# Moving output stores to another queue, and three smaller edits, in a planned attention and gated-convolution kernel

## The chip, the cores and the metric

The kernel runs on one core of a Trainium2 chip. The metric is the device time of one execution in microseconds (us); smaller is better. A core has the engines TensorE (PE; its weight loads are shown as PEld), VectorE (DVE), ScalarE (ACT), GpSimd (POOL) and SyncE (SP), each with its own queue of instructions that it takes strictly in order. SP, ACT and POOL also issue DMA transfers. The names SPq and POOLq stand for these queues.

## The reference

Two stages. The first is causal attention with a forgetting gate for 8 batches, 8 heads, 576 positions and head size 64:

```python
scores = scale * np.matmul(q, k.transpose(0, 1, 3, 2))
cum = np.cumsum(np.log(np.clip(f, 0.0001, 1.0)), axis=-1)
decay = cum[:, :, :, None] - cum[:, :, None, :]
scores = np.where(causal, -1000000000.0, scores + decay)
attn = softmax(scores);  x = attn @ v      # then (B, S, H * D) = (8, 576, 512)
```

The second is a gated feed-forward with a convolution over the sequence, 512 to 1024 to 512, for each batch:

```python
h = np.maximum(x @ w_in, 0.0)              # w_in 512 x 1024
conv_out = conv_w[0] * h[s-1] + conv_w[1] * h[s] + conv_w[2] * h[s+1]
out = (h * sigmoid(conv_out)) @ w_out      # w_out 1024 x 512
```

## The kernel before

**Units of work.** Attention goes by half batches `hb` of 4 heads (16 of them) and inside them by pairs `i` of 2 heads (32). For a half batch, `load_qk` (L110) loads Q and K with DMA transposes into tiles `stq` and `stk`, a ring of four: half batch `hb` takes the tile of `hb - 4` and waits until PE has used it. V is loaded in five transfers (`load_v`, L158). The tiles hold 16-bit halves of the fp32 inputs, and some of their partitions are used for other things: constants are put there by `fill` (L132) with DMAs from a tile of constants, and the cumulated log of the gate, the decay, as a high and a low bf16 part (`rows_of`, L139 and L141). The decay rows come from `kd`, a copy in DRAM of the tiles `khi_sb` and `klo_sb`, which hold one row for each head. `clamp` (L119) on DVE prepares other partitions; for Q of half batches from `CLAMPS` = 8 on, an additional fill of 48 rows takes the place of that clamp.

For each pair PE computes the scores (L293, with mask matmuls L299 and L325), ACT the exponentials (L305, L319, L333), PE the product with V ("PV", L351), and DVE the normalized result `xn` (`norm`, L362 and L364). When a batch's four pairs are through, `xn` is transposed to `xt`: for batches 0, 1 and 7 on PE (`xpose_pe`, L397, copied out of PSUM by ACT or DVE, L406 and L408), for the others by five DMA transposes on SP (`xpose`, L383).

The feed-forward goes by batch `g` and block `ff` of 128 of the 1024 inner columns: L420 on PE, `relu` (L433) on ACT, two steps of the convolution (L450, L452) on DVE, `tanh` or for the last batch sigmoid (L462, L460) on ACT, `gate` (L470, L468) on DVE. The second matmul (L482) takes chunks of 128 positions, nine for two batches. A chunk's result is put into an output buffer `ob` by ACT or DVE (`evac`, L506, L508); a buffer holds two chunks, and there are three buffers. `store` (L515, L517) writes them to the output with DMAs on SP. For the last batch the second matmul runs block by block into banks that attention no longer needs (`moe2_last`, L495); two chunks of the batch before it (those from `HELD` = 2 on) are computed after that.

**The order of the work.** Nothing reorders instructions at run time. A planner writes the order: each unit is a `task` with engines and estimated times, the tasks it comes after, a key (its due time), the ring or buffer that it takes and gives back, a lag until others may use its result, and DMA time. `play()` runs through an estimated clock and lets each engine take the ready task with the smallest key; the kernel is then emitted in that order. A task's give-back was counted 0.1 us after its issue, for DMAs too. `AHEAD` (4.0) limits how far score tasks may run ahead of the feed-forward, `QUEUED` (8.0) how much estimated DMA time SP may have queued.

```python
z = task({"SP": 0.55}, [x], key, lambda g=g, c=c, n=1 if single else 2: store(g, c, n),
         give=[("ob", y if c % 2 else x)] if c % 2 or c == 8 else [], lag=2.0, ...)
...
if give:
    heapq.heappush(heap, (end + 0.1, k, "give"))
```

**Weights.** `w_in` (L630) and `w_out` (L150) are loaded by POOL. So that they don't come too early, a store of one element by DVE (`hold`, L146) into the destination makes the DMA wait for it.

Of the kernel before, what the change touches and what calls it, by code (L numbers as in the profile page):

```python
# [18 lines left out]
def kernel(  # L19
# [115 lines left out]
    def rows_of(hb):  # L135

        tq, tk = stq_t[hb % RING], stk_t[hb % RING]
        c = slice(hb * HH, (hb + 1) * HH)
        nc.gpsimd.dma_start(tq[126:127, 0:HS], kd[0:1, c, :].rearrange("j h s -> j (h s)"))  # L139
        row = HS + 64  # L140
        nc.gpsimd.dma_start(bass.AP(tensor=tk.tensor, offset=int(tk.offset) + 96 * row, ap=[[2 * row, 2], [1, HS]]),  # L141
                            kd[:, c, :].rearrange("j h s -> j (h s)"))

    def hold(w):

        nc.vector.memset(w[0:1, 0, 0:1], 0.0)  # L146
# [360 lines left out]
        else:  # L507
            nc.vector.tensor_scalar(ob, ps, by, None, op0=ALU.mult)  # L508

    def store(g, c, n):  # L510

        r = (g - g % 2) * S + 128 * (c + 1 - n)
        ob = ob_of[g, c - c % 2]
        if n == 1:
            nc.sync.dma_start(outf[r:r + 128, :], ob[:, c % 2, :])  # L515
        else:
            nc.sync.dma_start(outf[r:r + 256, :].rearrange("(j p) c -> p j c", p=128), ob)  # L517

# [19 lines left out]
        nc.vector.memset(z[0:2, :], PAIR)  # L540
        nc.vector.memset(z[32:33, :], MINUS)

    CLAMPS, HALVES, LANDING = 8, 16, 3.0
    HELD = 2
    WAITS = ((3, 0), (3, 1), (4, 0), (4, 1))
    room = {"sc": 2, "O": 1, "mm": 2, "pm": 2, "xn": 2, "xt": 2, "u": 2, "ht": NHT,
            "hg": 2, "ob": 3}
# [7 lines left out]
    for hb in range(NHB):  # L555
# [4 lines left out]
        for s in range(2):  # L560
            if hb == 1:
                x = task({"ACT": 0.01}, [], -9, lambda: None, lag=(0.3, 3.8)[s])
            elif hb:
                last = x = task({"SP": 3.0}, ring, key + 0.1 * s, lambda hb=hb, s=s: load_qk(hb, 0, 4, s),
                                lag=LANDING, dma=3.1, behind=last)
            if hb:
                landed.append(x)
            if hb:
                t = (stq_t, stk_t)[s][hb % RING]
                rows = [(100, 14, 19)] if s else [(96, 15, 0)] + [(0, 48, 33)] * (hb >= CLAMPS)  # L570
                even.append(task({"POOL": 0.55 * len(rows)}, [t_fsrc, x], 2 * hb - 3.5,
                                 lambda t=t, rows=rows: [fill(t, *x) for x in rows],
                                 lag=4.0, dma=0.3 if s or hb < CLAMPS else 1.2))
            if hb and (s or hb < CLAMPS):
                even.append(task({"DVE": 0.9}, [x], (2 * hb - 3 if hb > 1 else -5) + 0.2 * s,
                                 lambda hb=hb, s=s: clamp(hb, s, 0, 4, 96)))
# [12 lines left out]
                x = task({"DVE": 0.1}, [even[1] if side == 0 else even[-1]], -9, lambda j=j: hold(w_out_f16[:, 2 * j:2 * j + 2, :]))  # L589
                t_wout.append(task({"POOL": 0.8}, [x], 2 * hb - 1.0, lambda j=j: load_w_out(j), lag=2.0, dma=1.7))  # L590
        if hb:
            t_rows[hb] = even + [task({"POOL": 1.1}, landed, 2 * hb - 3.6 if hb > 1 else -1.0,
                                      lambda hb=hb: rows_of(hb), lag=3.8)]
        else:
            t_rows[hb] = []
        for p in range(2):
# [4 lines left out]
        for p in range(2):  # L601
            i = 2 * hb + p
            if i == 1:
                t_rows[hb] = [t_second]
            if p == 0:
                x = t_second = task({"ACT": 0.01}, [], -9, lambda: None, lag=3.7) if i == 0 else None
                t_tail = x = task({"PE": 0.36}, t_rows[hb] + [x] * (i == 0), i + (0.02 if i else 0.65),
                                  lambda hb=hb: tail_scores(hb), take="sc")
                tail = task({"ACT": 0.36}, [x] + ([t_pv[i - 3, 1]] if hb >= 2 else []), i + 0.02,
                            lambda hb=hb: tail_exp(hb), give=[("sc", x)])  # L610
            exps = {}
            x = task({"PE": 0.9}, t_rows[hb], i + 0.1, lambda i=i: diag_scores(i), take="sc")
            t_qk[hb, p] = [t_tail, x]
            mask = task({"ACT": 1.02}, [x], i + 0.1, lambda i=i: diag_exp(i), take="pm", give=[("sc", x)])
            for s in range(2):
                x = task({"PE": 0.46}, t_rows[hb], i + 0.2 + 0.4 * s, lambda i=i, s=s: off_scores(i, s),
                         take="sc")
                t_qk[hb, p].append(x)
                exps[s] = task({"ACT": 1.02}, [x] + ([t_pv[i - 2, s]] if i >= 2 else []), i + 0.2 + 0.4 * s,
                               lambda i=i, s=s: off_exp(i, s), give=[("sc", x)])  # L620
            for s in range(2):
                t_pv[i, s] = task({"PE": 0.5}, [exps[s], mask, tail, t_cast[hb, 0], t_cast[hb, 1]]
                                  + ([t_pv[i, 0]] if s else []), i + 0.9 + 0.4 * s,
                                  lambda i=i, s=s: pv(i, s), take="O" if s == 0 else None,
                                  give=[("pm", mask)] if s else [])
            t_norm[i] = task({"DVE": 1.05}, [t_pv[i, 1]], i - 0.5, lambda i=i: norm(i),
                             take="xn" if i % PPB == 0 else None, give=[("O", t_pv[i, 0])])
            if i == 0:
                x = task({"DVE": 0.1}, [t_norm[0]], -9, lambda: hold(w_in_f16))
                t_win = task({"POOL": 1.0}, [x], -0.5, lambda: nc.gpsimd.dma_start(  # L630
                    w_in_f16, moe_w_in.rearrange("(cc p) ff -> p cc ff", p=128)), lag=2.0, dma=6.5)
        if hb % 2:
            norms = [t_norm[i - j] for j in range(PPB)]
            if b in (0,1,7):
                t_xt[b] = []
                for tb in range(NKB):
                    x = task({"PE": 0.27}, norms, i + 0.3 + 0.1 * tb, lambda b=b, tb=tb: xpose_pe(b, tb),
                             take="mm", also="xt" if tb == 0 and grp_of[b][1] == 0 else None, behind=x if tb else None)
                    if tb == 0:
                        t_xt0[b] = x  # L640
                    t_xt[b].append(task({"DVE": 0.4, "ACT": 0.57}, [x], i, lambda e, b=b, tb=tb: xpose_out(b, tb, e),
                                        give=[("mm", x)] + ([("xn", t_norm[i - 3])] if tb == NKB - 1 else [])))
            else:
                t_xt0[b] = task({"SP": 7.0}, norms, i + 0.5, lambda b=b: xpose(b),
                                take="xt" if grp_of[b][1] == 0 else None,
                                give=[("xn", t_norm[i - 3])], lag=2.8, dma=3.1)
                t_xt[b] = [t_xt0[b]]
# [5 lines left out]
    for g, (b0, nb) in enumerate(GROUPS):  # L653
# [3 lines left out]
        for ff in range(NFF):  # L657
# [16 lines left out]
            if ff == 0 and g % 2 == 0:  # L674
                t_hg = x
            t_tanh.append(x)
            t_gate[g, ff] = task({"DVE": 0.1 + n / 1800.0 if g == LAST else 0.2 + n / 1050.0}, [x], key - 1.5, lambda g=g, ff=ff: gate(g, ff),
                                 give=[("ht", t_m1[-nt])])
        t_exp = t_tanh if g == LAST - 1 else []
        done = [t_gate[g, ff] for ff in range(NFF)]  # L680
# [12 lines left out]
        for c in chunks:  # L693
            key = start[g + 1] + (start[g + 2] - start[g + 1]) * (c - chunks[0]) / len(chunks) + 5.0
            if g == LAST:
                x = t_m2[0] if t_m2 else x
            else:
                late = g == LAST - 1 and c >= HELD
                x = task({"PE": 1.73}, done + t_wout, key + 99 * late, lambda g=g, c=c: moe2(g, c), take="mm")
                if late:  # L700
                    t_late.append(x)
            t_m2.append(x)
            x = task({"DVE": 0.62, "ACT": 0.57}, [x] + ([y] if c % 2 else []), key - 2.0,
                     lambda e, g=g, c=c: evac(g, c, e), give=[("mm", x)] if g < LAST else [], take="ob" if c % 2 == 0 else None)
            single = c == 8 or g >= LAST - 1
            if c % 2 or single:
                z = task({"SP": 0.55}, [x], key, lambda g=g, c=c, n=1 if single else 2: store(g, c, n),
                         give=[("ob", y if c % 2 else x)] if c % 2 or c == 8 else [], lag=2.0, dma=0.45 if single else 0.9)
            y = x
        if g % 2:  # L710
            task({"SP": 0.01}, t_m2, key, lambda: None, give=[("hg", t_hg)])

    AHEAD, QUEUED = 4.0, 8.0

    def play():
        busy = {"PE": 11.5, "ACT": 12.0, "DVE": 12.0, "POOL": 14.0, "SP": 19.0}
# [16 lines left out]
        while len(started) < len(tasks):  # L733
# [11 lines left out]
            for e in ("PE", "ACT", "DVE", "POOL", "SP"):  # L745
# [3 lines left out]
                while ready[e]:  # L749
# [27 lines left out]
                    end = clock + engines[e]  # L777
                    busy[e] = end
                    heapq.heappush(heap, (end, -1, None))
                    if give:  # L780
                        heapq.heappush(heap, (end + 0.1, k, "give"))
                    if dma:
                        dma_free = max(dma_free, clock) + dma
                        end = max(end, dma_free) if e == "SP" else end + 2.5 + dma
                    heapq.heappush(heap, (end + lag, k, "done"))
                    break
                for x in kept:
# [1 line left out]
        return order, clock  # L789

    order, est = play()
    engine_of = {"DVE": nc.vector, "POOL": nc.gpsimd}
    for number, e in order:
        engines, fn = tasks[number][0], tasks[number][2]
        if fn.__code__.co_argcount > len(fn.__defaults__ or ()):
# [33 lines left out]
```

## Time and profile before

| what | value |
|---|---|
| median of 13 runs (lowest to highest) | 283.4 us (281.2 to 288.78) |
| the profiled execution: its time | 282.51 us |
| its span in the trace | 280.8 us, so 1.7 us lie around it |
| mean granted TensorE clock | 0.963 of full speed |
| busy: PE, DVE, ACT, POOL | 240.7, 219.4, 208.1, 50.6 us |
| output stores | 24, all issued by SP: 12 of 512 KB (4.4 us median to landing), 12 of 256 KB (2.2 us) |
| first scores of half batches 1, 2, 3 | 23.0, 41.1, 54.3 us |
| last PV result (`xn` of the last pair) | 238.1 us |

A row of the profile names a line, an engine, an operation, and tiles as out<-in. Busy time says how long an engine worked; "idle before" and the list of waits say what ended its waiting. The chain of work that ended last is followed back from the last instruction, at each step to what released it. Engines can be busy and still not set the time: what counts is which wait ends last in a stage.

### The profile page before, as it was taken

How to read it: one execution, taken by the hardware profiler on the slowest of the kernel's cores; microseconds unless marked ns; L12 is line 12 of the kernel's file. 1: busy time of each engine (PE TensorE's matmuls, PEld its weight loads, DVE VectorE, ACT ScalarE, POOL GpSimd, SP SyncE). 2: the span in 40 equal slices, each digit the busy share in tenths (PEclk: the TensorE clock that was granted, in tenths of full speed). 3: DMA queues.
4: the chain of work that ended last, by engine and by line, in shares of the span. 5: the costliest groups of instructions: out<-in, count | busy, mean ns of one | idle time of the engine just before them, and what ended most of it. 6: DMA issues, size and time to landing. Idle time of an engine off the chain costs nothing.

```text
span 280.8 us, 6414 instructions
## 1 busy us (share of the span) xinstructions
PE 240.7 (86%) x2480; PEld 162.2 (58%) x2502; DVE 219.4 (78%) x392; ACT 208.1 (74%) x347; POOL 50.6 (18%) x111
## 2 busy tenths in 40 slices
PE   2865779688999984999998479999999999799991
PEld 1344557467767663766676247776766666455540
DVE  5864548999999984699898358999879988989650
ACT  4082649699889993798997269899988899876632
POOL 4371203331233030321030303040020000000000
PEclk9997979999999998999999959999999999999997
DMA  8999999999999997999699969998995402101035
GB/s 129 207 205 156 222 194 227 179 225 201 166 180 197 184 212 125 218 196 229 127 224 232 240 143 235 210 215 156 159 262 170 142 0 77 75 4 75 37 131 206
DMA packets 134980, 47.53 MB, mean 169 GB/s; under 512 B 127858, under 2 KB 128882, under 8 KB 134950
## 3 DMA queue, kind: packets, MB, share of 16 engines
q1 hardware_dynamic: 130416, 40.72, 74.6%
q0 software_dynamic: 4208, 6.24, 10.7%
q8 instruction: 19, 0.31, 0.5%
q10 hardware_dynamic: 326, 0.17, 0.4%
q14 instruction: 11, 0.09, 0.1%
HBM read 14.01 MB, written 9.58 MB: 84 GB/s over the span
## 4 chain that ended last, share of the span: by engine, by line
PE 52%; DVE 11%; DMA 11%; ACT 11%; SPq 7%; issue 5%; POOL 2%; DVEq 0%; ACTq 0%; POOLq 0%
PE mm L420 17%; PE mm L482 13%; PE sc L293 10%; PE O L351 6%; SPq L383 4%; DMA stq<-in_q_dram 3%; DMA out_dram<-ob 3%; ACT po L319 3%; PE sc L495 2%; ACT pm L333 2%; PE sc L325 2%; DMA stk<-kd 2%; DVE u L452 2%; DVE u L450 2%; ACT hg L462 2%
## 5 line engine op out<-in xcount | busy, mean ns | idle before, releaser
L420 PE MATMUL mm<-xt,w_in_f 128*128 128x288 f16 x512 | 80.5, 293 | 11.2 <-ACT ob L506 5.4
L293 PE MATMUL sc<-stq,stk 128*128 128x128 bf16 (+3 forms) x576 | 67.0, 245 | 9.6 <-ACT pm L333 3.5
L433 ACT ACTIVATE ht<-mm 128x288 f16<-128x288 f32 x128 | 51.9, 417 | 18.7 <-PE mm L420 16.0
L319 ACT ACTIVATE po<-sc 128x1024 f16<-128x1024 f32 x64 | 64.5, 1030 | 1.6 <-PE sc L293 1.5
L420 PEld LDWEIGHTS <-w_in_f 128*128 128x128 f16 x512 | 48.2, 99 | 29.8 <-issue 10.1
L450 DVE SCALAR_TENSOR_TENSOR u<-ht,cwt 128x576 f32<-128x576 f16 x64 | 51.5, 811 | 13.4 <-ACT ht L433 12.1
L293 PEld LDWEIGHTS <-stk 128*128 128x128 bf16 x576 | 42.7, 100 | 31.3 <-issue 8.3
L482 PE MATMUL mm<-w_out_f,hg 128*128 128x512 f16 x248 | 59.1, 384 | 0.1
L452 DVE SCALAR_TENSOR_TENSOR u<-ht,cwt,u 128x576 f32<-128x576 f16 x64 | 51.4, 811 | 0.4
L470 DVE SCALAR_TENSOR_TENSOR hg<-hg,ht 128x576 f16<-128x576 f16 x56 | 41.6, 750 | 11.6 <-ACT hg L462 11.4
L462 ACT ACTIVATE hg<-u,cwt 128x576 f16<-128x576 f32 x56 | 43.4, 780 | 2.9 <-DVE u L452 2.8
L333 ACT ACTIVATE pm<-sc 128x1024 f16<-128x1024 f32 x32 | 32.8, 1024 | 12.9 <-PE sc L293 12.8
L482 PEld LDWEIGHTS <-hg 128*128 128x128 f16 x248 | 24.0, 99 | 25.3 <-issue 1.8
L351 PE MATMUL O<-va,po 128*128 128x65 f16 x640 | 37.0, 195 | 0.4 <-ACT po L319 0.2
L351 PE MATMUL O<-va,pm 128*128 128x65 f16 x256 | 31.5, 195 | 3.4 <-DVE xn L364 3.4
L132 POOL DMA_DIRECT2D stq<-consts x23 | 12.4, 543 | 118.1 <-DMA stq<-in_q_dram 55.2
L351 PEld LDWEIGHTS <-po 128*128 128x128 f16 x640 | 31.1, 99 | 1.4 <-ACT po L319 0.7
L351 PEld LDWEIGHTS <-pm 128*128 128x128 f16 x256 | 24.7, 99 | 6.3 <-DVE xn L364 4.3
L506 ACT ACTIVATE ob<-mm 128x512 f32<-128x512 f32 x27 | 16.0, 598 | 16.3 <-DMA out_dram<-ob 9.8
L364 DVE TENSOR_TENSOR xn<-O,rc 128x640 f16<-128x640 f32 x32 | 26.4, 825 | 1.1
L325 PE MATMUL sc<-trib,identb 128*128 128x512 bf16 x42 | 16.1, 384 | 1.1 <-ACT po L319 1.0
L119 DVE TENSOR_SCALAR stk<-stk,lim 96x2304 uint16<-96x2304 uint16 (+1 forms) x17 | 14.2, 835 | 1.4 <-DMA stk<-in_k_dram 1.2
(105 smaller groups left out, 182.9 us busy)
## 6 DMA issues: line engine op xcount, KB each, us to landing
vf<-in_v_dram SPq DMA_DIRECT2D x64, 128.0 KB, 3.9
out_dram<-ob SPq DMA_DIRECT2D x12, 512.0 KB, 4.4
out_dram<-ob SPq DMA_DIRECT2D x12, 256.0 KB, 2.2
stq<-consts POOLq DMA_DIRECT2D x8, 216.0 KB, 4.6
vf<-in_v_dram SPq DMA_DIRECT2D x16, 64.0 KB, 4.8
w_in_f<-in_moe_w_in_dram POOLq DMA_DIRECT2D x1, 1024.0 KB, 10.6
w_out_f<-in_moe_w_out_dram POOLq DMA_DIRECT2D x4, 256.0 KB, 6.4
stq<-consts POOLq DMA_DIRECT2D x15, 67.5 KB, 3.6
```

The lines of the kernel that those rows point to most:

```text
L293: nc.tensor.matmul(sc, stk_t[hb % RING][:, k0:k0 + 128], stq_t[hb % RING][:, q0:q0 + w], start=start, stop=stop, skip_group_check=True)
L319: nc.scalar.activation(p_of[i, s][:, 0:1024], sc_of.pop((i, s)), AF.Exp, scale=SCALE)
L333: nc.scalar.activation(p_of[i, 2], sc_of.pop((i, 2)), AF.Exp, scale=SCALE)
L351: nc.tensor.matmul(O[:, s, 65 * Q:65 * (Q + 1)], w, va[:, h, m, :], start=(m == 0), stop=(m == Q))
L364: nc.vector.tensor_tensor(xo, Ov[:, :, :, 0:64], rc.unsqueeze(3).broadcast_to((128, 2, NKB, 64)), op=ALU.mult)
L420: nc.tensor.matmul(ps[:, 0:w], w_in_f16[:, cc, 128 * ff:128 * (ff + 1)], xt[:, cc, w * t:w * (t + 1)], start=(cc == 0), stop=(cc == NCC - 1))
L433: nc.scalar.activation(ht[:, 0, HT_0 + w * t:HT_0 + w * (t + 1)], ps[:, 0:w], AF.Relu)
L450: nc.vector.scalar_tensor_tensor(u, hl, cwt[:, ff, 0:1], hc, op0=ALU.mult, op1=ALU.add)
L452: nc.vector.scalar_tensor_tensor(u, hr, cwt[:, ff, 1:2], u, op0=ALU.mult, op1=ALU.add)
L462: nc.scalar.activation(hv, u, AF.Tanh, scale=cwt[:, ff, 2:3])
L470: nc.vector.scalar_tensor_tensor(hv, hv, 1.0, hc, op0=ALU.add, op1=ALU.mult)
L482: nc.tensor.matmul(ps, chunk(g, ff, c), w_out_f16[:, ff, :], start=(ff == 0), stop=(ff == NFF - 1))
```

## The change

- Stores of all batches but the last (`g` up to `POOLED` = 6) are issued by POOL. The planner gives them 0.8 us there.
- In the planner a DMA task gives back what it holds at its estimated landing plus its lag, no longer 0.1 us after its issue.
- The decay rows of half batch 1 are taken from `khi_sb` and `klo_sb` in SBUF by three DMAs, no longer from `kd` by two.
- The hold of `w_in` is part of the first pair's `norm` task, no longer a task by itself.
- Batch 2, too, is transposed on PE: batches 0, 1, 2 and 7.
- `CLAMPS` is 5, so half batches 5 to 7 get the 48-row fill for Q in place of the clamp.
- Numbers of the plan: `AHEAD` 3.0, `QUEUED` 5.0, the lags of fills and rows 4.0, and the keys of `norm`, `gate` and `evac`.

```diff
@@ rows_of
+        if hb == 1:
+            nc.gpsimd.dma_start(tk[96:97, 0:HS], khi_sb[c, :])
+            nc.gpsimd.dma_start(tk[98:99, 0:HS], klo_sb[c, :])
+            nc.gpsimd.dma_start(tq[126:127, 0:HS], khi_sb[c, :])
+            return
@@ store
-    def store(g, c, n):
+    def store(g, c, n, eng):
...
-            nc.sync.dma_start(outf[r:r + 128, :], ob[:, c % 2, :])
+            eng.dma_start(outf[r:r + 128, :], ob[:, c % 2, :])
...
@@ the plan
-    CLAMPS, HALVES, LANDING = 8, 16, 3.0
-    HELD = 2
+    CLAMPS, HALVES, LANDING = 5, 16, 3.0
+    HELD, POOLED = 2, 6
...
-            t_norm[i] = task({"DVE": 1.05}, [t_pv[i, 1]], i - 0.5, lambda i=i: norm(i),
+            t_norm[i] = task({"DVE": 1.05}, [t_pv[i, 1]], i - 1.5, lambda i=i: norm(i) if i else [norm(i), hold(w_in_f16)],
...
-                x = task({"DVE": 0.1}, [t_norm[0]], -9, lambda: hold(w_in_f16))
-                t_win = task({"POOL": 1.0}, [x], -0.5, lambda: nc.gpsimd.dma_start(
+                t_win = task({"POOL": 1.0}, [t_norm[0]], -0.5, lambda: nc.gpsimd.dma_start(
...
-            if b in (0,1,7):
+            if b in (0,1,2,7):
...
-            t_gate[g, ff] = task(..., [x], key - 1.5, ...
+            t_gate[g, ff] = task(..., [x], key - 0.2, ...
...
-            x = task({"DVE": 0.62, "ACT": 0.57}, [x] + ([y] if c % 2 else []), key - 2.0,
+            x = task({"DVE": 0.62, "ACT": 0.57}, [x] + ([y] if c % 2 else []), key - 4.0,
...
-                z = task({"SP": 0.55}, [x], key, lambda g=g, c=c, n=1 if single else 2: store(g, c, n),
+                z = task({"SP": 0.55} if g > POOLED else {"POOL": 0.8}, [x], key,
+                         lambda e, g=g, c=c, n=1 if single else 2: store(g, c, n, e),
...
-    AHEAD, QUEUED = 4.0, 8.0
+    AHEAD, QUEUED = 3.0, 5.0
...
-                    if give:
-                        heapq.heappush(heap, (end + 0.1, k, "give"))
+                    freed = end + 0.1
                     if dma:
                         dma_free = max(dma_free, clock) + dma
                         end = max(end, dma_free) if e == "SP" else end + 2.5 + dma
+                        freed = end + lag
+                    if give:
+                        heapq.heappush(heap, (freed, k, "give"))
```

More of the change, by code (lines that the diff above doesn't have):

```diff
@@ L514, in store @@
         if n == 1:
-            nc.sync.dma_start(outf[r:r + 128, :], ob[:, c % 2, :])
+            eng.dma_start(outf[r:r + 128, :], ob[:, c % 2, :])
         else:
-            nc.sync.dma_start(outf[r:r + 256, :].rearrange("(j p) c -> p j c", p=128), ob)
+            eng.dma_start(outf[r:r + 256, :].rearrange("(j p) c -> p j c", p=128), ob)
     tasks, left, due, next_of = [], [], [], []
@@ L572 @@
                                  lambda t=t, rows=rows: [fill(t, *x) for x in rows],
-                                 lag=4.0, dma=0.3 if s or hb < CLAMPS else 1.2))
+                                 lag=LANDING + 1.0, dma=0.3 if s or hb < CLAMPS else 1.2))
             if hb and (s or hb < CLAMPS):
@@ L591 @@
         if hb:
-            t_rows[hb] = even + [task({"POOL": 1.1}, landed, 2 * hb - 3.6 if hb > 1 else -1.0,
-                                      lambda hb=hb: rows_of(hb), lag=3.8)]
+            t_rows[hb] = even + [task({"POOL": 1.1 if hb > 1 else 1.6}, landed, 2 * hb - 3.6 if hb > 1 else -9 if hb > 1 else -1.0,
+                                      lambda hb=hb: rows_of(hb), lag=LANDING + 1.0)]
         else:
@@ L676 @@
             t_tanh.append(x)
-            t_gate[g, ff] = task({"DVE": 0.1 + n / 1800.0 if g == LAST else 0.2 + n / 1050.0}, [x], key - 1.5, lambda g=g, ff=ff: gate(g, ff),
+            t_gate[g, ff] = task({"DVE": 0.1 + n / 1800.0 if g == LAST else 0.2 + n / 1050.0}, [x], key - 0.2, lambda g=g, ff=ff: gate(g, ff),
                                  give=[("ht", t_m1[-nt])])
@@ L791 @@
     order, est = play()
-    engine_of = {"DVE": nc.vector, "POOL": nc.gpsimd}
+    engine_of = {"DVE": nc.vector, "POOL": nc.gpsimd, "SP": nc.sync}
     for number, e in order:
```

## The prediction

> **What bounds the kernel now.** I read the engine busy times in stretches of 10 us first, then the waits, then the chain of work. Columns of the stretches: PE, PEld, DVE, ACT, POOL busy (instructions), granted TensorE clock, DMA share, GB/s.
>
> ```profile
> 50.00:60.00 10.00, 6.95 (x73) 4.76 (x72) 9.46 (x20) 7.44 (x14) 4.30 (x7) 1.00 1.26 194
> ...
> 90.00:100.00 10.00, 9.99 (x111) 6.52 (x110) 9.82 (x17) 9.54 (x16) 2.51 (x5) 1.00 1.12 200
> 100.00:110.00 10.00, 5.37 (x80) 3.89 (x79) 6.44 (x13) 6.60 (x9) 1.02 (x2) 1.00 0.84 137
> 110.00:120.00 10.00, 9.94 (x96) 7.24 (x95) 6.42 (x10) 7.32 (x14) 2.56 (x5) 0.83 1.19 223
> ...
> 150.00:160.00 10.00, 6.92 (x74) 4.43 (x74) 5.95 (x10) 5.18 (x9) 2.69 (x5) 1.00 0.98 224
> 160.00:170.00 10.00, 7.01 (x46) 4.01 (x46) 5.63 (x9) 5.71 (x9) 0.00 (x0) 0.66 0.80 178
> 170.00:180.00 10.00, 9.95 (x129) 7.54 (x129) 8.26 (x15) 9.11 (x18) 2.67 (x5) 1.00 1.17 221
> ```
>
> PE is busy for 9.6 to 10 us in nearly every stretch from 60 to 240: it is the bound there. It has two holes, at 100 to 110 (4.6 us lost) and at 150 to 170 (6.1 us lost). After both the granted clock falls, to 0.83 and 0.66, so each hole costs twice: idle time, then slow matmuls. The first 60 us lose more, but to a chain of single steps at the start that the change hardly touches.
>
> What ends each hole is in the waits (total us, times, longest):
>
> ```profile
> ACT ob L506 <- DMA out_dram<-ob: 9.8, 3, 6.4
> ...
> PE mm L420 <- ACT ob L506: 5.4, 2, 5.1
> ...
> PE mm L420 <- DMA xt<-xn: 4.2, 3, 2.5
> ```
>
> The chain over the second hole (start, us, what) tells how:
>
> ```profile
> 150.81 2.64 SPq L110
> 153.51 0.57 SPq L158
> 154.14 0.50 SPq L158
> 154.68 2.16 SPq L158
> 156.88 0.51 SPq L158
> 157.43 0.62 SPq L158
> 158.16 4.09 DMA out_dram<-ob
> 162.34 0.61 ACT ob L506
> 162.99 1.12 PE mm L420 x4
> ...
> 165.78 2.87 PE mm L482 x8
> 169.97 1.73 PE mm L482 x8
> ```
>
> An output store stands on SP behind a K load (L110) and five V loads (L158). Only when it lands at 162.25 is an output buffer free; ACT, in order, sat 6.41 us on the eviction L506, and PE 5.1 us behind ACT. The next rows are slow: eight L482 matmuls take 2.87 us here and 1.73 later.
>
> The first hole has the same queue and another passenger: batch 2's last norm starts at 90.69, but its five DMA transposes (L383) are issued at 100.95, behind half batch 8's loads. PE waits 2.53 and 1.33 us for them, 3.9 in all. From 100 to 170 SP waits little for other engines: it has simply more to issue than time.
>
> **Part 1, stores to POOL, buffers given back at landing in the plan.** Of 24 stores 19 go to POOL; the five of the last batch stay on SP. There they share the order with fills and decay rows, not with loads.
> - Idle gone: 5.1 us.
> - Slow clock gone, by the rows of 162.99 to 168.65 against the same groups nearby: L420 x4 1.12 against 0.49, scores x4 0.85 against 0.44, PV x15 0.83 against 0.49, L482 x8 2.87 against 1.73. Together 0.63 + 0.41 + 0.34 + 1.14 = 2.5.
> - Sum 7.6. Lower end 0: if batch 4's transposes, issued at 158.91 over 6.72 us, become the next wait, all of it can come back. Upper end 10.6 (ACT's two such waits, 6.41 + 1.74, and the 2.5). I take 7.6, since part 2 makes those transposes earlier by up to 7.5 us and each store moved saves SP another 0.54.
> - POOL pays 19 issues. The nearest row is w_out, as many rows of 2 KB from the same queue: 0.91 us each, 17 us on an engine busy 18%. POOL's order is the risk (rival 3), not its load.
>
> **The Trainium skill** speaks against this. DMA: Bandwidth & Descriptors, section "Issuing engines are not separate DMA queues", says that all queues end on the same 16 DMA engines, so another issuing engine saves issue time only. By that the gain would be the 24 - 5 issues, 19 x 0.54 = 10 us of SP time, and nothing of transfer time. The trace says that in-order issue is what hurts: the store itself took 4.09 us, the loads' issue ahead of it 7.3. SBUF — State Buffer (the box on DVE and SWDGE) says that POOL cannot write descriptors while DVE holds the shared port; here POOL's small issues spread from 0.50 to 1.07 us, so I count that at most at 0.6 us an issue, off the path.
>
> **Part 2, batch 2's transposes on PE.** The wait of 3.9 goes, and with it the slow rows at 109.71 to 114: L420 x4 0.96 against 0.49, scores x4 0.85 against 0.44, PV x15 0.82 against 0.49, L420 x8 1.53 against 0.98, together 1.8. Added: 20 transposes on PE; L397 shows 60 of them with 5.0 us busy and 3.0 us of waits, a third of which is 2.7. Net gain 5.7 - 2.7 = 3.0. Their five evictions (0.40 on DVE, 0.53 on ACT) are 2.0 to 2.7 us on engines at 9.5 to 9.8 of 10 around 90 us. **Part 3** pays for that: three clamps of Q (half batches 5 to 7) leave DVE, 3 x 0.81 = 2.4, and become POOL fills of 216 KB (0.5 us issue, 4.6 to landing). I set these two against each other at 0, within 0.5 either way.
>
> **Part 4, start.** Half batch 1's rows come from SBUF in three DMAs, not two from DRAM. Now the second is issued at 19.40 and lands 5.21 later, at 24.6, and PE waits 1.4 for it. The third would be issued at about 19.9; the rows of the same kind (khi, klo from POOL) land after 3.9 to 4.6: 23.8 to 24.5. Gain 0.1 to 0.8; I take 0.3, as DVE waits for V until 24.64 anyway. The first weights are held only by the first norm (ends at 21.99), no longer by a line at 25.20, so their issue moves from 25.57 to about 22. They land after 10.6, so at 32.6 instead of 36.2, while the first L420 at 38.22 waits for the transposes' copies: worth 0, cover 2 us before and more after.
>
> **Part 5, the end.** The last two evictions wait 1.66 us for a buffer and end at 277.2. In the new order the two late chunks of the last-but-one batch are evicted ahead of bank O, but their stores are POOL's. Evicted at about 275.6, with 0.6 to issue, they land 2.2 (SP's 256 KB) to 6.4 us (w_out, 256 KB on POOL) later: 278.4 to 282.6, against 277.2 + 0.4 + 2.2 = 279.8 now. Cost -1.4 to +2.8; I take +0.5.
>
> **Part 6, the plan's other numbers.** Keys and look-ahead reorder PE, ACT and DVE, and more of the last two batches' MoE work is left for after the last PV: 100 L420 against 84 and three more chunks of L482. There PE was busy 8.0 to 10.0 of 10 and DVE 6.8 to 9.1, so it is the same work elsewhere. No row prices new small waits. Bounds: -2.0 (the hole of 240 to 250, if filled) to +5.7 (one new hole like the first). I take +2.4, nearer the middle because 12 us of removed waiting rarely finds every other engine ready.
>
> **Sum.** -7.6 - 3.0 + 0 - 0.3 + 0.5 + 2.4 = -8.0. Against the profiled execution, 282.51 (span 280.8 and 1.7 around it), this gives 274.5. The median of the runs is 283.4, 0.9 above that execution, so 275.4; I predict 275.4.
>
> **Rivals.**
> 1. Transposes take the stores' place: SP issues L383 still behind the loads (9 us after the norm for batch 3, 13 for batch 4). For: the new SP order keeps them there. Against: by batch 4 SP is lighter by batch 2's 7.5 us and three stores, 9 us; and the new PE order has 14 to 17 us of matmuls between the last PV of batches 3 to 6 and their first L420 (columns at the rate of L482's rows, 512 in 0.216 us). Part 1 then brings 2 instead of 7.6: 281.0.
> 2. DVE becomes the bound: it has 219 us and runs at 9.5 to 9.8 between 50 and 100. Half of the gain stays: 279.4.
> 3. POOL's order (slower). A store waiting for its eviction stands ahead of the decay rows of half batches 6, 10, 12 and 15, and a store behind a Q fill waits as long as that fill does, up to 15.1 us now. Rows are needed 5.0 us after landing for half batch 6 (79.46 + 4.3 against 88.83), 7.6 to 14 for the others; evictions of a pair come about every 10 us into three buffers. From a delay of 5 us (rows) or over 15 us (buffers) PE stops again, at the second hole's price of 7.6. One stop gives 283.0, and from the second the change is slower: 275.4 + 15.2 = 290.6. It decides if the plan's clock and the chip's drift apart by more than those leads. Against: the plan frees buffers 2 us after an estimated landing, so it is careful here.
> 4. Gains and costs cancel (part 6 and part 5 at their worse ends, +5.7 and +2.8 for 2.4 and 0.5, and a little less from part 1): 275.4 + 5.6 = 281.0 at least, 283 with part 1 at 5.6.
>
> **Chances.** Forecast 0.53 (own range 271 to 278.5), rival 2 0.17, rival 1 0.09, rival 4 0.07, rival 3 0.14. Faster by over 0.5% (about what a measurement of this kernel tells from no change) holds the forecast, rivals 1 and 2: 0.79; within 0.5% 0.07; slower 0.14. The low end takes part 1 at its upper end, parts 2 and 4 as taken and the rest at nothing: 283.4 - 10.6 - 3.0 - 0.3 = 269.5. The high end takes in rivals 1, 2 and 4 and one stop of rival 3 (275.4 + 7.6 = 283.0), with the 1.4 of the measurement on top: 284.5. It leaves out the second stop.
>
> **What would show it.** Right: no ACT wait for out_dram over 1 us before 240, PE over 9.5 of 10 at 100 to 110 and 150 to 170 and the clock there at 1.00; the five POOL issues around half batches 6 and 10 without PE waits on stk or stq. Wrong: PE waiting for xt at the first L420 of batches 3 to 6 (rival 1), PE waiting for ACT or DVE with DVE over 9.5 (rival 2), PE waiting for kd rows or ACT for ob (rival 3), a last landing after 4 us on POOL (part 5).

## The result, and the profile after

The changed kernel is slightly slower: a median of 287.78 us (11 runs) beside 283.73 (48 runs of the kernel before), a ratio of **1.0091, 95% interval 1.0047 to 1.0135**. Measured once more later it was 1.0120 (1.0003 to 1.0238). The prediction was 275.4 us (269.5 to 284.5), with 0.79 on faster. Ratios in this document compare undisturbed executions of both kernels, so they need not be the quotient of two medians; the profiled execution of the changed kernel (290.9 us, span 289.1) is one of its longer ones, and where a reading rests on it alone this is said. A ratio of 0.01 is about 2.8 us here. Each experiment was measured beside the kernel before on one chip, but not all on the same chip (four in all); a difference between the ratios of two chips is less certain than its size suggests. Five lines were added, so L383, L420, L482, L506 of before are L388, L425, L487, L511 now; runs with a line more in `store` show the stores at L521 and L523 instead of L520 and L522.

First the busy times in stretches, as in the prediction (PE, PEld, DVE, ACT, POOL busy, granted clock, DMA share, GB/s):

```profile
90.00:100.00 10.00, 8.53 (x112) 6.33 (x113) 7.47 (x13) 9.28 (x15) 3.71 (x6) 1.00 1.20 173
100.00:110.00 10.00, 8.67 (x114) 6.95 (x115) 9.30 (x18) 7.14 (x14) 2.70 (x5) 1.00 1.14 246
110.00:120.00 10.00, 9.89 (x129) 7.42 (x130) 9.48 (x17) 9.40 (x18) 3.19 (x5) 1.00 1.16 192
130.00:140.00 10.00, 7.00 (x54) 4.11 (x53) 6.31 (x13) 5.05 (x7) 2.20 (x4) 0.89 1.08 244
150.00:160.00 10.00, 9.89 (x121) 7.46 (x122) 9.54 (x15) 9.47 (x17) 3.21 (x6) 1.00 1.06 170
160.00:170.00 10.00, 7.57 (x69) 4.57 (x69) 7.12 (x13) 7.34 (x12) 0.85 (x2) 1.00 1.08 223
190.00:200.00 10.00, 5.60 (x33) 3.05 (x33) 6.05 (x10) 4.73 (x8) 0.00 (x0) 0.79 1.19 187
270.00:280.00 10.00, 8.56 (x40) 3.54 (x37) 3.76 (x7) 5.30 (x9) 1.60 (x3) 1.00 0.42 160
280.00:289.10 9.10, 0.00 (x0) 0.00 (x0) 0.00 (x0) 0.00 (x0) 0.03 (x1) 0.56 0.15 59
```

Two things are to be seen. The holes of before (PE 5.37 at 100 to 110, 6.92 and 7.01 at 150 to 170) have become smaller: 8.67 at 100 to 110, 9.89 at 150 to 160, and 7.57 at 160 to 170. But there are two new ones, at 130 (7.00) and 190 (5.60). And the last row: nine microseconds in which no engine computes.

The waits (total us, times, longest) say what the holes are. No ACT or DVE wait for `out_dram` is left; the wait for the transposes has grown from 4.2 us to 9.7:

```profile
PE mm L425 <- DMA xt<-xn: 9.7, 5, 3.9
...
PE mm L425 <- ACT ob L511: 0.4, 2, 0.2
```

The chain (start, us, what) over the hole at 130, and the median landing of a transpose, counted from its issue (last column, us), before and now:

```profile
131.55 0.98 SPq L388
132.57 1.26 SPq L388
133.88 4.17 DMA xt<-xn
138.18 1.12 PE mm L425 x4
```

```profile
xt<-xn SPq DMA_TRANSPOSE x25, 2.6
xt<-xn SPq DMA_TRANSPOSE x20, 4.0
```

These are the transposes of batch 3. The same kind of rows stands at 160.66 to 168.79 for batch 4, where the output store stood before, and at 189.23 to 198.20 for batch 5.

The end, in the timeline of the changed kernel (start, us, engine, what):

```profile
278.60 0.60 ACT L511 ACTIVATE ob<-mm 128x512 f32<-128x512 f32 x1 [1.08 <-PE mm L487]
279.09 0.59 ACT L511 ACTIVATE ob<-O 128x512 f32<-128x512 f32 x1
279.49 0.54 POOL L520 DMA_DIRECT2D out_dram<-ob  x1 [1.14 <-ACT ob L511]
```

and the last row of its chain of work:

```profile
279.46 0.56 POOLq L831
```

Below, of the kernel before:

```profile
274.50 3.08 SPq L515 DMA_DIRECT2D out_dram<-ob  x4
276.13 1.09 ACT L506 ACTIVATE ob<-mm 128x512 f32<-128x512 f32 x2 [1.66 <-DMA out_dram<-ob]
```

Before, the last store was issued on SP until 277.6, and the span ends at 280.8: 3.2 us later. Now the last one is issued on POOL until 280.0 and lands at about 282, but the span ends at 289.1, 9.1 us after the issue. The chain stops at POOL's queue: nothing that the trace names comes after it. This reading doesn't rest on one execution alone: the second profile of the changed kernel (the last experiment) has the same 9.1 us.

### The profile page after: what moved, and what is told of

Its sections match the earlier page's. It is cut to its first block, busy times and chain, and to the rows that moved or that the text cites. A ratio compares the mean times of both kernels' runs of the same rounds, so it can differ in the third digit from the quotient of the medians.

```text
span 289.1 us, 6478 instructions
## 1 busy us (share of the span) xinstructions
PE 242.6 (84%) x2499; PEld 163.9 (57%) x2522; DVE 221.3 (77%) x397; ACT 207.5 (72%) x344; POOL 66.5 (23%) x134
## 4 chain that ended last, share of the span: by engine, by line
PE 53%; DMA 14%; DVE 10%; SPq 6%; ACT 5%; issue 4%; POOL 3%; POOLq 0%; ACTq 0%; DVEq 0%
PE mm L425 17%; PE mm L487 12%; PE sc L298 11%; PE O L356 7%; DMA stk<-in_k_dram 5%; SPq L388 4%; DMA vf<-in_v_dram 4%; DMA xt<-xn 4%; PE sc L500 2%; PE sc L330 2%; DVE xn L369 2%; DMA stq<-khi_sb 2%; ACT ht L438 2%; DVE u L455 2%; DVE hg L475 1%
## 5 line engine op out<-in xcount | busy, mean ns | idle before, releaser
L425 PE MATMUL mm<-xt,w_in_f 128*128 128x288 f16 x512 | 81.5, 295 | 11.6 <-DMA xt<-xn 9.7
L298 PE MATMUL sc<-stq,stk 128*128 128x128 bf16 (+3 forms) x576 | 70.7, 251 | 10.1 <-DMA stk<-in_k_dram 2.5
L438 ACT ACTIVATE ht<-mm 128x288 f16<-128x288 f32 x128 | 52.3, 417 | 27.8 <-PE mm L425 24.9
L425 PEld LDWEIGHTS <-w_in_f 128*128 128x128 f16 x512 | 48.3, 100 | 31.1 <-issue 10.1
L298 PEld LDWEIGHTS <-stk 128*128 128x128 bf16 x576 | 44.6, 102 | 30.5 <-issue 10.1
L487 PE MATMUL mm<-w_out_f,hg 128*128 128x512 f16 x248 | 57.8, 379 | 0.0
L487 PEld LDWEIGHTS <-hg 128*128 128x128 f16 x248 | 23.5, 98 | 24.2 <-issue 0.2
L132 POOL DMA_DIRECT2D stq<-consts x26 | 13.9, 537 | 97.3 <-DMA stq<-in_q_dram 52.9
L522 POOL DMA_DIRECT2D out_dram<-ob x12 | 9.3, 774 | 56.9 <-ACT ob L511 19.5
L511 ACT ACTIVATE ob<-mm 128x512 f32<-128x512 f32 x23 | 13.8, 600 | 11.3 <-PE mm L487 9.9
L367 DVE RECIPROCAL rc<-O 128x10 f32<-128x10 f32 x32 | 6.9, 216 | 13.5 <-PE O L356 13.1
```

The source lines that it names most:

```text
L298: nc.tensor.matmul(sc, stk_t[hb % RING][:, k0:k0 + 128], stq_t[hb % RING][:, q0:q0 + w], start=start, stop=stop, skip_group_check=True)
L425: nc.tensor.matmul(ps[:, 0:w], w_in_f16[:, cc, 128 * ff:128 * (ff + 1)], xt[:, cc, w * t:w * (t + 1)], start=(cc == 0), stop=(cc == NCC - 1))
L438: nc.scalar.activation(ht[:, 0, HT_0 + w * t:HT_0 + w * (t + 1)], ps[:, 0:w], AF.Relu)
L487: nc.tensor.matmul(ps, chunk(g, ff, c), w_out_f16[:, ff, :], start=(ff == 0), stop=(ff == NFF - 1))
```

## The experiments

Four theories are named in the expectations. **1**: the transposes of batches 3 to 5, issued on SP behind loads, take the place of the store's wait. **2**: stores on a queue of their own run beside the transposes and slow them. **3**: the plan's new keys and look-ahead do the harm. **4**, formed after the first four runs: a store that POOL issues near the end holds the program open.

**Before's order, only the queue changed** (19 stores on POOL, nothing planned anew):

```diff
-            nc.sync.dma_start(outf[...], ob)
+            eng.dma_start(outf[...], ob)          # eng = nc.gpsimd if g <= 6 else nc.sync
```

> The kernel before with its own plan and order; only the 19 stores of batches 0 to 6 are issued by POOL, at the places the order gives them. Theory 1 (the transposes of batches 3 to 5 stand behind the loads on SP and take the place of the store's wait): ACT's waits for out_dram before 240 us are gone, PE waits more for xt at batch 4, and 1 to 4 us are won, 279.5 to 282.5. Theory 2 (stores on a queue of their own run beside the transposes and slow them): transposes land later than before in every batch, no gain or 1 to 4 us lost, 284 to 288. Theory 3 (the plan's new keys and look-ahead do the harm): the full 5 to 7.6 us of the first estimate are won, 276 to 278.5.

Measured: 1.0369 (1.0305 to 1.0433). So the queue alone costs 10 us in this order: PE's wait for `xt` goes from 4.2 to 11.7 us, and a transpose lands after 4.1 us instead of 2.6. PE's wait for the decay rows (`stk<-kd`) also grows, from 1.7 to 4.9 us, and the time from the last issue to the end of the span from 3.2 to 8.8.

```profile
PE mm L420 <- DMA xt<-xn: 11.7, 6, 3.3
xt<-xn SPq DMA_TRANSPOSE x25, 4.1
```

**The changed order, all stores on SP** (emitted with `eng = nc.sync`, the plan unchanged):

> The changed kernel with its own plan and order; only the queue is put back: all stores are issued by SP. Theory 1: the transposes stand behind loads and stores, xt waits stay or grow by 0.5 us a store, 0 to 3 us slower than the changed kernel, 286 to 290. Theory 2: xt lands earlier, 2 to 4 us faster than the changed kernel, under 284. Theory 3: as the changed kernel within 1.5 us.

Measured: 0.9895 (0.9849 to 0.9941), 2% better than the changed kernel. With the first run this says that it is the queue that makes it slower. But PE's wait for `xt` is the same as in the changed kernel:

```profile
PE mm L425 <- DMA xt<-xn: 9.7, 4, 5.6
```

So the wait that was seen in the changed kernel doesn't tell the two queues apart, and speaks against theory 2 as the whole reason. (Further profiles of the changed order, below, have 5.5 to 8.4 us with stores on POOL.) The profile shows one thing more: ACT and DVE never wait for `out_dram` in it, though every store is on SP. In the new order that wait is gone without the new queue. All this led to the look at the end.

**No stores but the last batch's:**

```diff
+        if g <= 6:
+            return
```

> The changed kernel without its 19 POOL stores: only the last batch's output is written. Theory 1: PE still waits over 8 us for xt, time within 2 us of the changed kernel except for the stretch at the end. Theory 2: the waits for xt fall under 4 us and landing of a transpose from 4.0 to below 3 us, time 4 us or more below the changed kernel. Theory 3: as theory 1.

Measured: 0.9571 (0.9509 to 0.9633). PE is over 9.8 of 10 in the stretches of 10 us from 120 to 180, and a transpose lands after 2.6 us.

```profile
PE mm L425 <- DMA xt<-xn: 2.7, 2, 2.0
```

Against the same order with all stores on SP this is 3.2%, 9 us: what the 19 stores cost altogether on SP. SP's order of loads and transposes is the same here, so theory 1 alone, which has PE still wait over 8 us, falls; the expectation of theory 2 came true. But the wait is about as long with the stores on SP as on POOL, so it goes with the stores and not with their queue. This run has no long end, as its last stores are SP's.

**The changed kernel with before's keys, `AHEAD` 4.0 and `QUEUED` 8.0:**

```diff
-    AHEAD, QUEUED = 3.0, 5.0
+    AHEAD, QUEUED = 4.0, 8.0     # and the keys of norm, gate and evac
```

> The changed kernel with the keys of norm, gate and evac, AHEAD and QUEUED as before; stores on POOL, give-back at landing, batch 2 on PE, CLAMPS 5, the new start. Theory 3: the xt waits of batches 3 to 5 fall under 4 us and the time to 276 to 281. Theory 1: the waits stay, since SP's order of loads and transposes is the same, 284 to 287. Theory 2: the same, 284 to 288.

Measured: 1.0291 (1.0228 to 1.0353). Theory 3 falls: in this plan the new numbers bring 2%.

Then theory 4, on the four stores of batch 6 (`g == 6`), two of which are the last on POOL.

**The changed order, batch 6 stored by SP:**

```diff
+        eng = nc.sync if g == 6 else eng
```

> The changed kernel in its own order, but the four single stores of chunk group 6 (the last ones on GpSimd, two of them after 277 us) are issued by SP; the other 15 stay on GpSimd. Theory 4 (the end): a store issued by GpSimd near the end holds the program open; in the changed kernel's profile the last landing is at about 282 us and the span ends at 289.1, 7 us on, where the kernel before ends about 1 us after its last landing. By it the tail shrinks to 1 to 2 us and the time falls by 5 to 6 us: 0.987 to 0.992 of the kernel before, the same as with all stores on SP (0.9895). Theory 2 (the stores of the middle, on a queue of their own, slow the transposes): nothing much changes, 1.005 to 1.012, and the median landing of a transpose stays at 4.0 us.

Measured: 0.9856 (0.9752 to 0.9960): four DMAs on another queue, 2.4% or 6.6 us. 0.9856 is just under theory 4's range, which the interval holds; theory 2's is outside it. The end shrank less than theory 4 had it (1 to 2 us): in the profile the last store on SP is issued until 272.7 and the span ends at 276.5, 3.8 us later.

```profile
L523 POOL DMA_DIRECT2D out_dram<-ob x12: 710/750/1117, 80.5 to 249.5; - x12
L521 SPq DMA_DIRECT2D out_dram<-ob x9: 331/356/407, 252.4 to 272.4; - x9
L521 POOL DMA_DIRECT2D out_dram<-ob x3: 572/573/826, 131.6 to 250.9; - x3
```

(Line, engine, count: duration in ns min/median/max, first and last start in us.) POOL's last store is at 250.9; by then its queue has 25 us left, and costs nothing at the end.

**The converse: all stores on SP, only the very last of batch 6 on POOL:**

```diff
-        eng = nc.sync
+        eng = nc.gpsimd if (g, c) == (6, 3) else nc.sync
```

> The changed kernel's own order with all stores issued by SP (0.9895 of the kernel before), but the very last store of group 6 issued by GpSimd: one DMA of 256 KB on the other queue. Theory 4: that one DMA brings the whole tail back, plus 5 to 6 us: 1.008 to 1.013, with idle engines for 6 to 7 us after the last landing. Theory 2: one store at the end is beside no transpose; 0.985 to 0.993.

Measured: 1.0117 (1.0066 to 1.0168) against 0.9895 (0.9849 to 0.9941) without it: 2.2%, 6.3 us, for one DMA of 256 KB. (The 0.9895 is from another chip; on the chip of this run the changed order with batch 6 on SP had 0.9856, 2.6% less.) Its timeline ends so, and the span ends at 285.0:

```profile
276.38 0.59 ACT L511 ACTIVATE ob<-O 128x512 f32<-128x512 f32 x1
276.77 0.58 POOL L521 DMA_DIRECT2D out_dram<-ob  x1 [71.46 <-ACT ob L511]
277.00 0.33 SPq L521 DMA_DIRECT2D out_dram<-ob  x1
```

Both stores land within 3 us (2.9 on POOL, 2.1 on SP), at 279.7 and 279.1; then nothing happens for 5 us.

**Before's order, POOL for batches 0 to 5 only:**

> The kernel before in its own order, its 15 stores of groups 0 to 5 on GpSimd, those of group 6 on SP (with group 6 on GpSimd too it was 1.037). Theory 4: 6 us less than that, about 1.015 to 1.018; if the end is all, the rest goes too and it is 1.00. Theory 2: 1.030 to 1.037, transposes at 4 us, PE's waits for xt above 10 us. Between the two, the part over 1.00 is what the stores of the middle cost.

Measured: 1.0237 (1.0099 to 1.0374), span's end 3.8 us after SP's last issue, 8.8 with batch 6 on POOL. The interval still holds 1.0369, so the times alone don't show what the end costs in this order; the two profiles show 5 us of it. What is left, 2.4%, is the middle: here theory 2 or 1 holds too. The chain shows it (first two rows: batch 3 in the kernel before; then this run at batches 3 and 4). Of before's holes the store is gone, and the transposes stand in its place, landing later from their issue:

```profile
133.80 1.27 SPq L383
135.11 2.35 DMA xt<-xn
```

```profile
131.41 1.26 SPq L383
132.72 5.77 DMA xt<-xn
...
162.25 1.28 SPq L383
163.57 5.02 DMA xt<-xn
```

**The changed kernel, all batches transposed by PE** (batches 0 to 7 instead of 0, 1, 2 and 7, planned anew):

> The changed kernel with the transposes of batches 3 to 6 also made by TensorE (20 DMA transposes fewer; the plan is made anew with them), stores on GpSimd. Theory 1 or 2 (slow or late transposes are what the stores' gain was lost to): PE's 9.7 us of waits for xt go, at a price of 20 x 0.27 = 5.4 us of PE: about 4 us less than the changed kernel, 0.993 to 0.998. Theory 4: the transposes' waits are not what made it slower, and the end's 6 us stay; PE's extra work shows: 1.005 to 1.03.

Measured: 1.0006 (0.9944 to 1.0068), between the two expectations: the waits for `xt` end, the tail stays (9.2 us from POOL's last issue to the span's end of 284.0).

**The same with batch 6 stored by SP:**

> The changed kernel with all transposes of xn on TensorE (1.0006 of the kernel before) and the four stores of group 6 issued by SP. Theory 4, now shown for one store at the end: the tail of 5 to 6 us goes here too, 0.978 to 0.985. If the tail and the transposes' waits share the same time, less than the 6 us comes back: 0.985 to 0.995.

Measured: 0.9883 (0.9800 to 0.9966). The tail goes here as well. It is no better than with the DMA transposes (0.9856): what PE no longer waits it spends on transposing. Whether slower DMA transposes cost anything net is not told by this pair.

**Where the tail runs from: batch 6 on SP, but the last batch's first store on POOL:**

```diff
-        eng = nc.sync if g == 6 else eng
+        eng = nc.sync if g == 6 else nc.gpsimd if (g, c) == (7, 4) else eng
```

> The changed kernel with group 6 on SP (0.9856), but the last batch's first store, which is issued some 5 us before the last one, on GpSimd. It asks from where the tail runs. Theory 4a: the program ends no sooner than some 9 us after GpSimd's last store (9.1 in the changed kernel, 7.7 with a single store), whatever else runs: 0 to 1.5 us later than with group 6 on SP, 0.985 to 0.992. Theory 4b: a store of GpSimd's that is still young at the end adds its 5 to 6 us after everything else: 1.005 to 1.012.

Measured: 0.9922 (0.9874 to 0.9970), as theory 4a has it and below 4b. The profile is plainer than the time:

```profile
L521 SPq DMA_DIRECT2D out_dram<-ob x8: 332/368/807, 253.4 to 273.2; - x8
L521 POOL DMA_DIRECT2D out_dram<-ob x4: 562/569/578, 133.6 to 268.8; - x4
```

The span ends at 278.6: 9.2 us after POOL's issue at 268.8 to 269.4, and 5.1 after SP's last. So in these runs the program ends about 9 us after POOL's last store, or some 3.5 after SP's, whichever is later.

**Single edits in the old plan.** Batch 2 on PE alone:

> The kernel before with one edit, batch 2 transposed by TensorE; the plan is made anew. Part 2 of the prediction: 3.0 us and half of a clamp's price back, 0.987 to 0.992. If the hole at 100 to 110 only moves to the next batch's transposes: 0.997 to 1.005.

Measured: 1.0218 (1.0140 to 1.0297), 6 us worse. The hole at 100 to 110 is gone (PE 9.82), but new ones stand at 50 to 60 (4.94, 6.95 before), 130 to 140 (6.68) and 170 to 180 (7.02). Both expectations missed. Give-back at landing alone:

> The kernel before with one edit, the plan's give-back of a DMA task at its landing; the stores stay on SP. If the wait of 6.4 us for an output buffer came from the plan's reckoning, this alone removes it: 0.975 to 0.985. If the store is late because SP issues it behind the loads, whatever the plan reckons: the wait for out_dram stays or turns into an early stop of the evictions, 0.995 to 1.01.

Measured: 0.9928 (0.9869 to 0.9986), 2.0 us better; between the expectations. ACT's longest wait for `out_dram` falls from 6.4 to 2.4 us without any store leaving SP (DVE, which had none, has one of 3.3).

**The rest of the forecast.** The changed kernel with batch 6 on SP and batch 2's transposes back on SP:

> The changed kernel with group 6 stored by SP (0.9856) and batch 2's transposes back on SP, as before; the plan is made anew. As the prediction's part 2 has it, this loses 3 us: 0.994 to 0.999. As its trial in the old plan would have it (batch 2 on TensorE alone made the kernel 1.0218), it gains: 0.96 to 0.98.

Measured: 1.0023 (0.9952 to 1.0093), against 0.9856 (0.9752 to 0.9960) with them on PE: 1.7%, 4.7 us, in the direction of the prediction, with intervals that just overlap. The new keys, `AHEAD` and `QUEUED` in the kernel before:

> The kernel before with one edit, the plan's keys of norm, gate and evac, AHEAD 3.0 and QUEUED 5.0 of the changed kernel. Part 6 of the prediction took these at a cost of 2.4 us: 1.004 to 1.013. If they help by themselves as much as they do in the changed kernel, where the old numbers made 1.0291 of 1.0091: 0.975 to 0.985. If they only fit what is planned with them: 0.995 to 1.02.

Measured: 1.0141 (1.0053 to 1.0229): by themselves they cost 4 us, while in the changed plan the old ones cost 5.7. And the changed kernel again:

> The changed kernel itself, once more, beside the other two. By what was measured of it: 1.005 to 1.013, and about 9 us from the last store's issue on GpSimd to the end of the span.

Measured: 1.0120 (1.0003 to 1.0238). This execution took 282.94 us (span 281.2): the waits for `xt` are 5.5 us, PE has one hole between 60 and 240 (5.55 at 180 to 190), and the tail is the same, 9.1 us from the end of POOL's last issue at 272.11:

```profile
271.57 0.54 POOL L520 DMA_DIRECT2D out_dram<-ob  x1 [1.14 <-ACT ob L511]
```

What the first profile shows of the holes at 130 and 160 is thus partly its own; the tail is in both.

## Why the prediction was wrong

**Part 5 is the step that failed, and after it part 1.** Part 5 took the landing of the last store for the end of the program: "they land 2.2 (SP's 256 KB) to 6.4 us (w_out, 256 KB on POOL) later: 278.4 to 282.6", hence -1.4 to +2.8, taken as +0.5. The landing was right: 2.7 us after issue, at about 282, and the sign that the prediction had named for this part, a landing after 4 us, didn't show. But the program didn't end there. With a late store on POOL the end costs 6.3 us (one store, the rest on SP) or 6.6 (four), more than twice the upper bound. With the measured size in place of +0.5 the sum becomes -8.0 + 5.8 = -2.2, still faster, so this term is not the whole of the error: the ratio of 1.0091 is +2.6. The other 4.8 us were, as far as the runs tell, expected of part 1 and didn't come.

No row of before could have priced it as such, since there POOL's last DMA was long before the end (its busy time is 0.00 from 210 on). That was the signal: an engine that has issued nothing late is given the last DMA, and the prediction bounded this by landing times alone instead of asking what the end of a program waits for on that queue.

**Part 1** came out near the end that it had named as its lower one, "if batch 4's transposes, issued at 158.91 over 6.72 us, become the next wait, all of it can come back". The wait for the output buffer did go, in both profiles of the changed kernel. But with the tail taken out, the changed kernel without part 2 is 1.0023: parts 1, 3, 4 and 6 together bring nothing that can be measured, where -5.5 was taken for them. The reason for taking 7.6, that the transposes would be earlier and SP lighter, failed: PE waits for them at batches 3 to 5 of the changed kernel (9.7 and 5.5 us in its two profiles, 4.2 before), and in before's own order 11.7 us, where they took 4.1 us to land instead of 2.6. The rule that the prediction weighed (the Trainium skill, DMA: Bandwidth & Descriptors, "Issuing engines are not separate DMA queues": another issuer saves issue time only) stood nearer to this than the prediction's objection to it: all stores on SP gives 0.9895, POOL for the 15 earlier ones 0.9856, no difference that can be told. And with all stores on SP the new order has no wait for `out_dram` either, so it was not the queue that removed it. The give-back, the planner's part of part 1, brings 2.0 us alone.

**Rival 1** had the right mechanism (PE waiting for `xt` at the first L425 of batches 3 to 5) and the wrong end: 281.0 is near what the changed kernel would be without its tail (0.9856 of 283 is 279). **Rival 3** was on the right side, but its mechanism wasn't seen: PE's waits for the decay rows (`stk<-kd`) are 0.4 us in the changed kernel, 1.7 to 2.1 before. With the stores on POOL in before's own order they were 4.9 (2.3 with batch 6 on SP). **Rival 4**, gains and costs cancel, came nearest in kind; it had part 5 at +2.8. **Rival 2** is not what decided: DVE runs over 9.5 with PE below 8 in one stretch, 50 to 60 (9.96 and 6.89), where it was 9.46 and 6.95 before.

**Part 2**: forecast -3.0, measured -4.7 in the changed plan, and +6.2 in the old one. The hole that it was to fill was filled in both; what the new plan does elsewhere decided.

**Part 6**: the bounds of -2.0 to +5.7 hold the +4.0 that the numbers cost alone, but not the -5.7 that they bring in the changed plan. The term has no value of its own.

**Part 4**: the rows of half batch 1 were foreseen at 23.8 to 24.5. The third DMA was issued at 19.91, as foreseen, and landed 4.99 later:

```profile
19.91 4.99 DMA stq<-khi_sb
25.45 0.63 PE sc L298 x4
```

That is 24.9, so no gain instead of 0.3. But in the second profile of the changed kernel the same DMA is issued at 18.95, lands after 3.1 us, and PE doesn't wait for it. The term is smaller than what it varies by. **Part 3** was not tried by itself; its clamps of that shape take 0.87 us each before, not 0.81, which mixes two shapes, so 2.6 in place of 2.4, within what it allowed.

**What stays open.** What the program waits for in the 6 us or so between POOL's last landing and the end: the trace shows no instruction there. And how PE's wait for `xt` divides between transposes that SP issues late and transposes that land late: in the changed order it is 8.0 and 9.7 us with all or all but one of the stores on SP, where a transpose lands after 2.6 and 2.9 us, 5.5 to 9.7 with 15 to 19 stores on POOL (3.0 to 4.0 us to land), and 2.7 without the stores. No run has the one without the other. Transposes issued from another queue were not tried.

## What to carry to other kernels

The last store before the end of a program belongs on the queue whose end is cheap: here GpSimd's queue should have had nothing in the last 9 us or so. Read the time between the last issue and the end of the span for each queue before any store is moved. In a kernel whose order a planner makes, one number changes the whole order (single edits here moved the time by -2 to +6 us, and changed sign in another plan), so test an edit in a fixed order first, by emitting the same order with one thing different, and price the plan's redrawing as an uncertainty of its own. When a stall on an in-order queue is removed, the next passenger of that queue takes its place, unless what stands ahead of it goes too.

## What the runs showed of the hardware

**A late DMA on GpSimd's queue holds the program for about 9 us after its issue.** From the end of the last store's issue to the end of the span: 9.1, 9.1, 9.1, 9.2, 9.2 and 8.8 us in six profiles whose end a POOL store decides, 7.7 with a single store on POOL; where SP's stores decide it is 3.1 to 3.8, in ten profiles. The Trainium skill (DMA: Bandwidth & Descriptors, "SWDGE vs HWDGE vs iDMA") says that plain transfers belong to SP or ACT, where hardware writes the descriptors, and GpSimd is for accumulating, casting or irregular ones. The runs agree for the last store, 6 us; for the 15 earlier ones in the changed order they show no difference (0.9856 against 0.9895).

**DMA transposes landed later when the stores came from another queue.** The median landing, counted from the issue, is 2.6 us in before's order and 4.1 in the two profiles of that order with stores on POOL. In the changed order it is 2.6 and 2.9 with all or all but one of the stores on SP, 2.6 without them, and 3.0 to 4.0 in four profiles with 15 to 19 stores on POOL. That the stores running beside them are the reason is likely, but not shown separately. The landing varies between executions of one kernel (4.0 and 3.4 in two profiles of the changed kernel), and with all stores on SP it is 3.2 to 3.3 in three orders that were planned anew, so it can't be taken as a price.
